# Batch 0's k load moved to the SyncE queue, v and q moved up on the GpSimd queue, in a fused attention and MLP kernel

## The chip, the cores and the metric

One core of one Trainium2 chip. The time is device microseconds of one execution; profiles and stretches are in microseconds from the start of the span. "Granted clock" is the share of TensorE's full clock that the throttle granted. In the profiles PE is TensorE, PEld its weight loads, DVE VectorE, ACT ScalarE, POOL GpSimd and SP SyncE. A "packet" is what one DMA record of the trace moves.

## The reference, cut to what matters

```python
# q, k, v: (8 batches, 8 heads, 576 positions, 64), float32
q_p, k_p = phi(q), phi(k)            # relu, times cos and sin of the position: 128 features
kv  = einsum('bhsf,bhsd->bhfd', k_p, v);  z = sum(k_p, axis=2)
num = einsum('bhsf,bhfd->bhsd', q_p, kv)
den = einsum('bhsf,bhf->bhs', q_p, z)[..., None] + 1e-06
x   = (num / den).transpose(0, 2, 1, 3).reshape(4608, 512)
out = relu(x @ w_in) ** 2 @ w_out    # w_in 512 x 2048, w_out 2048 x 512
```

Nothing of the MLP can start before batch 0's k, v and q have come in and gone through attention.

## The kernel before

576 positions are 4 x 128 and 64 more. Each of k, v and q of a batch is loaded as a main part (1 MB, 4 positions side by side per partition, runs of 1024 bytes in memory) and a "tail" for the last 64 positions (two pieces of 64 KB, runs of 256 bytes).

```python
def load(src, nm, b, eng, parts=1, tail_eng=None):
    main = inp.tile([P, H, J, D], F32, name=nm, tag=nm, bufs=2)
    tail = inp.tile([P, HH, D], F32, name=nm + "t", tag=nm + "t", bufs=2)
    for i in range(parts):
        js = slice(i * J // parts, (i + 1) * J // parts)
        eng.dma_start(out=main[:, :, js, :],
            in_=src[b, :, 0:MAIN, :].rearrange("h (p j) d -> p h j d", j=J)[:, :, js, :])
    for g in range(2):
        (tail_eng or eng).dma_start(out=tail[g * TAIL : (g + 1) * TAIL, :, :],
            in_=src[b, g * HH : (g + 1) * HH, MAIN:S, :].rearrange("h p d -> p h d"))
# ... cut ...
with tc.manual_schedule():
    load(k, "k", 0, nc.gpsimd, 1, nc.sync)
    constants()                               # on GpSimd: iota, identity
    load(v, "v", 0, nc.gpsimd, 1, nc.sync)
    load(q, "q", 0, nc.gpsimd, 2, nc.sync)
    warm(34)                                  # dummy matmuls of 128 x 512, for TensorE's clock
    for j in range(NS):
        att_k(0, j)                           # kp: VectorE (cos) and ScalarE (sin); j = 4 is the tail
    att_v(0, 0, nc.vector)                    # vext: cast of v to bf16
    att_v(0, 1, nc.scalar)
    att_v(0, 2, nc.vector); att_v(0, 3, nc.vector)
    att_v(0, J, nc.vector)                    # vextt, the tail
    for i in range(4):
        load_w1(i, 4)                         # w_in, on GpSimd, cast to bf16 under way
    # ... loads of batch 1, w_out, batch 2, on GpSimd ...
    att_kv(0, 0); att_kv(0, 1)                # kz: 32 matmuls, then 8 that need both tails
    att_feat(0, 0); att_feat(0, 1)            # qp
    att_kvz(0, nc.vector.tensor_copy)         # kvz: kz out of PSUM, needs all 40
    # ... q transposed, num, division, x transposed: xT ...
    for s in range(len(slots)):
        run(s)                                # slots 0 to 3: hps = xT with a quarter of w_in each
```

Each engine keeps this order.

## Time and profile before

| | before |
|---|---|
| time, median (range) of 4 runs | 289.06 us (288.83 to 289.29) |
| span of the profiled run, granted clock | 288.1 us, 0.999 |
| k, v landed (as the casts that wait for them start) | 8.5, 12.07 |
| vextt, kvz start | 13.13, 14.34 |
| first matmul with w_in (slot 0) | 18.51 |
| slot 3, which needs the last quarter of w_in | 25.87 |

How to read it: the page gives busy shares; the chain of waits, followed back from the end, says what the time consists of; the timeline gives start, length, engine, line, operation and, in brackets, the idle time before it and what ended that. "SPq" and "POOLq" are the queues' issues. The lines themselves stand in the prediction below. The profiled execution of this kernel (289.87 us) was slower than the four timed ones. Two paths meet at slot 3: w_in's last quarter, and batch 0's k, v, q through attention into slot 0.

### The profile page before, as it was taken

What the parts mean: (1) busy time and instruction counts of PE and PEld (TensorE: products, weight loads), DVE (VectorE), ACT (ScalarE), POOL (GpSimd) and SP (SyncE); (2) the same over time, 40 slices, a digit from 0 to 9 for tenths busy, and PEclk for the clock granted to TensorE, in tenths of its full rate; (3) what the DMA queues carried; (4) which work ended last, traced back from release to release, by engine and by line L of the source; (5) the groups of instructions that cost most, each with busy time, mean ns of one, the idle gap of its engine ahead of it and who ended that gap; (6) DMA issues with size and microseconds to landing.
All of it is one profiled execution on the core that took longest, in us unless ns stands there. A gap on an engine that the chain in (4) does not pass through costs nothing.

```text
span 288.1 us, 7331 instructions
## 1 busy us (share of the span) xinstructions
PE 278.9 (97%) x3064; PEld 235.9 (82%) x3070; DVE 204.0 (71%) x457; ACT 161.7 (56%) x245; POOL 42.5 (15%) x70
## 2 busy tenths in 40 slices
PE   8699999999999999999999999999999999999995
PEld 3378845888678888898998888888998888889884
DVE  0676774588698399787598776977677877547585
ACT  2675653479759759455882348834695461155210
POOL 8632605750000000000002000000000000000002
PEclk9999999999999999999999999999999999999999
DMA  5999995999658799899529985399809720300015
GB/s 170 343 207 288 322 266 170 369 371 277 91 96 208 142 300 228 219 260 245 167 80 207 333 181 164 94 264 293 231 7 233 118 46 3 136 12 2 0 75 146
DMA packets 74497, 53.04 MB, mean 184 GB/s; under 512 B 52032, under 2 KB 68928, under 8 KB 74464
## 3 DMA queue, kind: packets, MB, share of 16 engines
q1 hardware_dynamic: 63840, 26.09, 40.4%
q0 software_dynamic: 10480, 26.35, 30.0%
q8 instruction: 24, 0.39, 0.5%
q10 hardware_dynamic: 144, 0.13, 0.1%
q14 instruction: 9, 0.07, 0.1%
HBM read 36.70 MB, written 9.44 MB: 160 GB/s over the span
## 4 chain that ended last, share of the span: by engine, by line
PE 85%; DMA 6%; POOL 2%; DVE 2%; ACT 2%; issue 1%; POOLq 0%; ACTq 0%
PE hps L388 40%; PE ya L530 9%; PE yc L530 9%; PE yu L530 7%; DMA w1sb<-in_moe_w_in_dram 6%; PE yv L530 5%; PE num L315 3%; PE kz L243 3%; PE yps L461 2%; PE yps L437 2%; PE yh L437 2%; DVE ysb L542 1%; PE tq L289 1%; POOL w1sb L119 1%; DVE u L542 1%
## 5 line engine op out<-in xcount | busy, mean ns | idle before, releaser
L388 PEld LDWEIGHTS <-w1sb 128*128 128x128 bf16 x1344 | 113.4, 98 | 12.8 <-issue 2.0
L388 PE MATMUL hps<-xT,w1sb 128*128 128x256 bf16 (+1 forms) x1088 | 119.3, 266 | 0.8 <-ACT rt L396 0.2
L396 ACT ACTIVATE rt<-hps 128x1024 bf16<-128x1024 f32 x72 | 73.6, 1023 | 67.6 <-PE hps L388 46.3
L403 DVE TENSOR_TENSOR gT<-rt 128x1024 bf16<-128x1024 bf16 x64 | 44.0, 687 | 19.9 <-ACT rt L396 19.9
L530 PEld LDWEIGHTS <-gs 128*128 128x128 bf16 x480 | 46.8, 98 | 5.4
L415 POOL DMA_DIRECT2D out_dram<-ysb x14 | 7.6, 546 | 171.4 <-DVE ysb L542 144.9
L530 PEld LDWEIGHTS <-gT 128*128 128x128 bf16 x312 | 29.8, 98 | 3.4
L183 ACT ACTIVATE kp<-k,sin_col 128x512 bf16<-128x512 f32 x32 | 22.4, 717 | 5.2 <-DMA k<-in_k_dram 5.2
L329 DVE TENSOR_TENSOR x<-num,rden 128x512 bf16<-128x512 f32 x32 | 22.1, 691 | 1.1
L183 ACT ACTIVATE qp<-q,sin_col 128x512 bf16<-128x512 f32 x32 | 22.0, 719 | 0.8 <-DMA q<-in_q_dram 0.8
L325 DVE TENSOR_SCALAR den<-num 128x8 f32<-128x8 f32 (+1 forms) x40 | 6.5, 164 | 21.5 <-PE num L315 21.4
L526 DVE TENSOR_TENSOR gs<-gT 128x1024 bf16<-128x1024 bf16 x26 | 17.8, 684 | 0.0
L530 PE MATMUL ya<-w2t,gs 128*128 128x256 bf16 x120 | 15.6, 273 | 0.0
L530 PE MATMUL yu<-w2t,gs 128*128 128x256 bf16 x120 | 15.6, 273 | 0.0
L530 PE MATMUL yc<-w2sb,gs 128*128 128x256 bf16 x120 | 15.5, 273 | 0.0
L388 PE MATMUL hps<-xTt,w1sb 128*128 128x128 bf16 x256 | 15.1, 219 | 0.2 <-ACT rt L396 0.2
L173 DVE TENSOR_SCALAR qp<-q,cos_col 128x512 bf16<-128x512 f32 x32 | 15.0, 496 | 0.1
L173 DVE TENSOR_SCALAR kp<-k,cos_col 128x512 bf16<-128x512 f32 x21 | 10.0, 501 | 7.1 <-DMA k<-in_k_dram 7.1
L530 PE MATMUL yu<-w2sb,gs 128*128 128x256 bf16 x112 | 14.5, 273 | 0.0
L202 ACT CAST vext<-v 128x512 bf16<-128x512 f32 x23 | 14.1, 614 | 0.6 <-DMA v<-in_v_dram 0.6
L581 ACT COPY s<-yu 128x256 f32<-128x256 f32 x14 | 5.2, 372 | 15.3 <-PE yu L530 15.3
L530 PE MATMUL yc<-w2sb,gT 128*128 128x256 bf16 x104 | 13.5, 273 | 0.0
(98 smaller groups left out, 336.6 us busy)
## 6 DMA issues: line engine op xcount, KB each, us to landing
out_dram<-ysb POOLq DMA_DIRECT2D x14, 512.0 KB, 4.4
k<-in_k_dram POOLq DMA_DIRECT2D x4, 1024.0 KB, 8.6
v<-in_v_dram POOLq DMA_DIRECT2D x4, 1024.0 KB, 8.6
k<-in_k_dram SPq DMA_DIRECT2D x4, 1024.0 KB, 8.6
v<-in_v_dram SPq DMA_DIRECT2D x4, 1024.0 KB, 8.7
q<-in_q_dram SPq DMA_DIRECT2D x4, 1024.0 KB, 6.6
q<-in_q_dram POOLq DMA_DIRECT2D x3, 1024.0 KB, 12.2
w1sb<-in_moe_w_in_dram POOLq DMA_DIRECT2D x4, 512.0 KB, 14.7
```

What stands on the lines that cost most here:

```text
L173: nc.vector.tensor_scalar(out=dst[:, :, 0:D], in0=src, scalar1=0.0, scalar2=cos_col[:, j : j + 1], op0=ALU.max, op1=ALU.mult,)
L183: nc.scalar.activation(out=dst[:, :, D:F], in_=src, func=ACTF.Relu, scale=sin_col[:, j : j + 1])
L202: copy(out=vx[:, j, h0:h1, 0:D], in_=piece("v", b, j)[:, h0:h1, :])
L243: nc.tensor.matmul(out=kz[:, half, hh * E1 : (hh + 1) * E1], lhsT=lhsT, rhs=rhs, start=(j == 0 and hh == 0), stop=(j == J and hh == HH - 1),)
L315: nc.tensor.matmul(out=out, lhsT=lhsT, rhs=kvz[:, half * HH + hh, :], start=True, stop=True)
L329: nc.vector.tensor_tensor(out=x_of(b, j).rearrange("p (b k) (l d) -> p b k l d", b=n, l=2), in0=n4[:, :, :, 0:D].rearrange("p b (k l) d -> ...
L388: nc.tensor.matmul(out=out, lhsT=w1sb[:, kb, hb * P : (hb + 1) * P], rhs=rhs, start=(kb == 0), stop=(kb == KB - 1),)
L396: nc.scalar.activation(out=rt[:, :, :], in_=hps[:, :, :], func=ACTF.Relu)
L403: nc.vector.tensor_tensor(out=dst, in0=rt[:, :, :], in1=rt[:, :, :], op=ALU.mult)
L437: nc.tensor.matmul(out=ypss[b][tt], lhsT=gTs[b][:, hb, tt * P : (tt + 1) * P], rhs=w2sb[:, hb, :], start=(hb == 0), stop=(hb == HB - 1),)
L526: nc.vector.tensor_tensor(out=t[:, :, :], in0=in0, in1=in1, op=op)
L530: nc.tensor.matmul(out=acc, lhsT=lhs[:, hb, :], rhs=rhs[:, hb, :], start=(hb == 0), stop=(hb == HB2 - 1),)
```

## The change

Its intent: GpSimd needs about 1 us to issue a load, so k is issued by the idle SyncE instead, and v, q and w_in move up. All should land sooner, hence three fewer dummy matmuls.

```diff
     with tc.manual_schedule():
-        load(k, "k", 0, nc.gpsimd, 1, nc.sync)
+        load(k, "k", 0, nc.sync)
+        load(v, "v", 0, nc.gpsimd, 1, nc.sync)
         constants()
-        load(v, "v", 0, nc.gpsimd, 1, nc.sync)
         load(q, "q", 0, nc.gpsimd, 2, nc.sync)
-        warm(34)
+        warm(31)
```

The tails stay on the SyncE queue, but now they stand behind k's 1 MB.

## The prediction

> **What bounds the kernel now.** I read the page first (share of each engine, then the 40 slices), then the chain of waits, the timeline of the first 26 us, the stretches of the same time, and at last the trace's DMA packet records, counted by queue.
>
> ```profile
> span 288.1 us, 7331 instructions
> PE 278.9 (97%) x3064; PEld 235.9 (82%) x3070; DVE 204.0 (71%) x457; ACT 161.7 (56%) x245; POOL 42.5 (15%) x70
> ...
> PE 85%; DMA 6%; POOL 2%; DVE 2%; ACT 2%; issue 1%; POOLq 0%; ACTq 0%
> ```
>
> TensorE bounds all but the start. DMA and POOL together are 8% of the chain, and the chain's list shows them only in the first 26 us, which is the only part that the change touches:
>
> ```profile
> 1.28 1.05 POOL k L66
> 3.51 0.94 POOL v L66
> 4.45 1.75 POOL q L66 x2
> 6.21 2.20 POOL w1sb L119 x3
> 8.41 17.41 DMA w1sb<-in_moe_w_in_dram
> 25.87 1.92 PE hps L388 x16
> ```
>
> The chain blames the w_in load until 25.82. The timeline shows that a second path ends nearly as late: k, v and q of batch 0 must become the first transposed x before the first matmul with w_in at 18.51 can run, and from there TensorE is busy nearly without a gap up to 25.87 (0.2 us of wait for w_in, in the list of waits).
>
> ```profile
> 0.74 1.41 SPq L71 DMA_DIRECT2D kt<-in_k_dram  x2
> 1.20 9.10 PE L208 MATMUL wm<-zeros 128*128 128x512 bf16 x34 [1.20 <-DVE zeros L88]
> 2.20 1.28 SPq L71 DMA_DIRECT2D vt<-in_v_dram  x2
> 8.50 2.56 ACT L183 ACTIVATE kp<-k,sin_col 128x512 bf16<-128x512 f32 x4 [5.21 <-DMA k<-in_k_dram]
> 12.07 1.14 DVE L202 CAST vext<-v 128x512 bf16<-128x512 f32 x3 [1.19 <-DMA v<-in_v_dram]
> 12.55 1.13 PE L243 MATMUL kz<-vext,kp 128*128 128x65 bf16 x32 [2.26 <-DVE vext L202]
> 13.13 0.28 DVE L200 CAST vextt<-vt 128x256 bf16<-128x256 f32 x1
> 14.34 0.69 DVE L254 CAST kvz<-kz 128x520 bf16<-128x520 f32 x1
> 18.51 1.95 PE L388 MATMUL hps<-xT,w1sb 128*128 128x128 bf16 x32
> ```
>
> The dummy matmuls (wm) end at 10.3; TensorE then stands until v is cast. Both paths are fed by the 16 DMA engines:
>
> ```profile
> 2.00:4.50 2.50, 2.50 (x7) 0.91 (x6) 0.00 (x0) 1.23 (x3) 2.18 (x8) 1.00 0.56 117
> 4.50:7.00 2.50, 2.50 (x13) 1.18 (x12) 0.00 (x0) 0.00 (x0) 2.50 (x4) 1.00 0.99 347
> 7.00:8.50 1.50, 1.50 (x9) 0.68 (x7) 0.00 (x0) 0.00 (x1) 1.50 (x3) 1.00 1.06 278
> 8.50:13.50 5.00, 2.74 (x41) 1.64 (x39) 3.70 (x9) 3.58 (x6) 2.55 (x3) 1.00 1.04 380
> 13.50:23.50 10.00, 9.33 (x135) 7.63 (x133) 6.95 (x17) 7.26 (x12) 3.06 (x4) 1.00 1.24 210
> ```
>
> The last two columns are the DMA share and GB/s: the engines are half idle until 4.5 and full after it. (The 210 of the w_in stretch counts bf16 bytes written; twice that is read.)
>
> **What the Trainium skill says.** "DMA: Bandwidth & Descriptors", section "Queues, rings and completion order": each DMA engine goes round robin between the queues with work, at packet granularity. The trace agrees. By queue and size its records give (GpSimd queue: 4096-byte packets; SyncE queue: 256-byte ones for tails, 1024-byte ones for k, v and q):
>
> ```
> us            GpSimd packets        SyncE packets
> 9.0 to 11.0   182 of 4096 B         187 of 256 B      v and q against q's tail
> 165.2-166.0   60 of 4096 B          63 of 1024 B      an output against v of batch 6
> packet alone: 4096 B 160 ns, 1024 B 46 ns, 256 B 18 ns, w_in (1024 B written) 98 ns
> ```
>
> One for one in number, so the queue with the small packets gets a quarter of the bytes or less. Same page, "Issuing engines are not separate DMA queues": another issuing engine only saves issue time. The trace agrees: an issue costs POOL 0.9 to 1.05 us and the bytes still take 2.5 to 3 us per MB. Same page, "Specifications": the first byte comes after about 1 us from GpSimd and 0.6 us from SyncE. Here it is longer but in the same order: tail issued at 0.74, first packet 2.2; k issued at 1.28, first packet 3.4. "TensorE: Matmul & The Clock Gate", "What's actually happening": an idle window of about 3.4 us drops the clock to half. The trace has a 2.26 us gap and keeps its clock at 1.00; no longer gap is there to test it.
>
> **The change, part by part.**
> Removed: k's issue on POOL (1.05 us; k is replaced by v at the same 1.28), and 3 of the 34 dummy matmuls (0.21 us each at the end, 0.65 us; they end at 9.65). Off the path in itself: they ended 2.25 us before they were needed.
> Moved up: v's issue from 3.51 to 1.28, q's and w_in's by 0.94 us. The order of instructions confirms that nothing else moves on POOL, and that TensorE only loses the three.
> Moved over: k's 1 MB to the SyncE queue, in front of all six tail pieces, as 1024 packets of 1024 bytes (64 per engine) instead of 256 of 4096 (16 per engine).
>
> Gain if nothing interferes: k's packets start at about 2.2 instead of 3.4. The engine time until q is done is tails 1536 x 18 ns / 16 = 1.7, k 64 x 0.046 = 2.9, v and q 2 x 16 x 0.16 = 5.1; it was 9.4 with k in large packets, so k costs 0.4 more. Idle share won back in 2.0 to 4.5: 0.44 x 2.5 = 1.1. Net 0.7 to 0.8 us on both paths, and so on the whole.
>
> Loss by round robin. A SyncE load of k in batch 4, issued at 97.66 with no rival, ran at 126 GB/s for its first 2 us (98.5 to 100.5) and 357 after. So by 4.5, when v's packets run at full rate, I take 0.35 MB of k as done: 43 of 64 packets per engine are left. Then:
> v, 16 rounds of 0.16 + 0.046 = 0.205: 3.3 us, to 7.8 (v lands near 9, before 12.04). q the same: to 11.1. k has 11 left, against w_in: 11 x (0.098 + 0.046) = 1.6, to 12.7; with about 1 us to the semaphore, k lands near 13.6, before 8.4.
> The tails stand behind k. Two of k, 32 rounds of 0.098 + 0.018 = 0.116: 3.7 us, to 16.4. Two of v: to 20.1, landing near 20.8, where vextt began at 13.13 before.
> Then vextt 0.28, two casts of q 0.88, so kvz starts near 22.0 instead of 14.34: +7.6. The first w_in matmul would be at 26 instead of 18.5. TensorE would stand from 9.65 to about 17, so its clock may fall: under 1 us more. w_in lands at its old time and takes no part. In the trace before, v's tails slipped through in a dip of the other queue (about 500 packets in 7.0 to 8.0); if they do so again, some 1 to 4 us come back. Estimate of this case: +6.5, range +3 to +9.
>
> **The rivals.**
> (A) k gets through before v is up, the tails slip through the dip between two loads. For: v's first packets were slow (3.4 to 4.5 in the case of k); the lowered count of dummy matmuls says that the author expects an earlier start. Against: the counts above. Result 289.2 - 0.8 = 288.4.
> (B) full round robin as worked out: 289.2 + 6.5 = 295.7. For: two places in the trace with one for one. Against: between 4.8 and 6.6 v's tails stood still beside k at all, so the rule isn't all that is at work.
> (C) k is late by 2 to 4 us only, or k is in time and the tails alone are late: kz waits for its last 8 matmuls. About +3, 292.
> (D) an issue on SyncE delays later work there: its queue has nothing else until 34 us. Nothing.
>
> **Range and chances.** A 0.35, B 0.40, C 0.25: mean 0.35 x 288.4 + 0.40 x 295.7 + 0.25 x 292 = 292.2; I say 292.5 as B can go higher. Range 288.0 to 297.0. 2% slower is 295.0: three quarters of B and a little of C, 0.36. 2% faster is 283.4: there are not 5.8 us to be won in this stretch, 0.02. The rest, 0.62, is within 2%.
>
> **What would show it.** In the timeline: the start of kp (8.50 now; near 13.6 in B, under 8 in A), of the first vext, of vextt (13.13; near 20 in B), of kvz, and of the first w_in matmul (18.51; 26 in B, 17.7 in A). In the packet counts: k's and v's packets one for one between 4.5 and 11. In the waits: in B, ACT and DVE wait for k for 10 us and for the tails after it; in A, the wait for w_in before 25.87 stays. The rest of the trace must be the same, shifted. I am wrong if the shift arises after 30 us, or if k lands late and the span doesn't move.

## The result, and the profile after

The changed kernel: 292.37 us, median of 4 (291.52 to 293.0), against 289.06. The ratio is 1.0113 (95% interval 1.0082 to 1.0143). A ratio is the mean time of one kernel's fast runs over that of the other's in the same rounds, so not quite the ratio of the medians quoted. That is 3.3 us slower, within the 2%. The profiled run (291.97 us, a span of 290.2) was one of its faster ones, and the profiled run of the kernel before one of its slower ones, so the two profiles lie only 2.1 us apart.

The chain of waits of the changed kernel, in order of time (start, length, what):

```profile
3.35 11.68 DMA vt<-in_v_dram
...
15.13 0.31 DVE vextt L200
...
15.48 0.40 PE kz L243 x8
...
21.23 1.79 PE hps L388 x32
...
28.11 1.75 PE hps L388 x16
```

Where the w_in load stood, there is now the load of v's tail: 64 KB that land 11.7 us after their issue. Most of that is waiting in the queue, behind k until 5.7 and then behind three other tail pieces; the four landed at 6.5, 11.1, 13.2 and 15.0. The timeline of the changed kernel:

```profile
0.74 0.45 SPq L66 DMA_DIRECT2D k<-in_k_dram  x1
1.25 1.38 SPq L71 DMA_DIRECT2D kt<-in_k_dram  x2
2.67 1.32 SPq L71 DMA_DIRECT2D vt<-in_v_dram  x2
6.36 2.56 ACT L183 ACTIVATE kp<-k,sin_col 128x512 bf16<-128x512 f32 x4 [3.08 <-DMA k<-in_k_dram]
11.17 0.35 DVE L173 TENSOR_SCALAR kpt<-kt,cos_col 128x256 bf16<-128x256 f32 x1 [1.69 <-DMA kt<-in_k_dram]
11.44 1.13 DVE L202 CAST vext<-v 128x512 bf16<-128x512 f32 x3
15.13 0.30 DVE L200 CAST vextt<-vt 128x256 bf16<-128x256 f32 x1 [2.56 <-DMA vt<-in_v_dram]
16.13 0.69 DVE L254 CAST kvz<-kz 128x520 bf16<-128x520 f32 x1
21.07 1.95 PE L388 MATMUL hps<-xT,w1sb 128*128 128x128 bf16 x32
24.90 0.76 POOL L126 DMA_DIRECT2D w2sb<-in_moe_w_out_dram  x1 [1.78 <-DMA w1sb<-in_moe_w_in_dram]
```

k came in at 6.3 instead of 8.4. The issue of w_out waits for the last quarter of w_in and so shows its landing: it started at 26.10 before and at 24.90 now. (The trace's semaphore events say 25.82 and 24.61.) So for k and v the intent worked: they landed 2.1 and 2.4 us sooner than in this profile of the kernel before, 1.6 us sooner each than in that of run 1. For w_in it isn't shown: in run 1, with the loads as before, the issue of w_out started at 24.91 too. And little of v's gain came through: vext stands behind kpt on VectorE, which waited for k's tail, so it began at 11.44 (before: 12.07, run 1: 11.26). Above all, vextt starts at 15.13 instead of 13.13, TensorE waits 2.4 us for it between the 32nd and the 33rd matmul of kz, and slot 0 starts 2.56 us later. Slot 3 starts at 27.95 instead of 25.87, 2.1 later; it no longer waits for w_in.

The stretches (columns: length, then busy time and count of PE, PEld, DVE, ACT, POOL, then granted clock, DMA share, GB/s). First the kernel before from 27.9 to its end:

```profile
27.90:288.10 260.20, 255.27 (x2825) 219.79 (x2827) 189.34 (x417) 147.46 (x223) 28.42 (x45) 1.00 0.68 177
```

Then the changed one, from 2.1 us later to its end, and two stretches of its start:

```profile
29.98:290.20 260.22, 255.53 (x2830) 219.76 (x2827) 189.27 (x417) 147.46 (x223) 26.38 (x42) 1.00 0.66 173
...
13.00:16.00 3.00, 0.63 (x13) 0.50 (x10) 0.87 (x3) 0.41 (x1) 0.61 (x1) 0.90 1.23 196
16.00:20.00 4.00, 3.77 (x39) 2.99 (x39) 2.96 (x9) 2.40 (x4) 1.54 (x2) 0.65 1.24 203
...
15.38:18.79 3.41, 3.09 (x33) 2.69 (x33) 2.46 (x7) 1.21 (x3) 0.90 (x1) 0.50 1.23 200
```

After slot 3 the two executions last equally long: the whole difference arises before. And TensorE's clock falls there, just where its work is on the path. The 0.65 is a mean over 4 us: the trace's clock record has 0.50 from 15.38 to 18.79 and 1.00 on either side.

The trace's packet records, counted by queue, show why the tail was late:

```
changed kernel, us         GpSimd packets           SyncE packets
before v's first packet    none (v's first: 5.35)   971 of k's 1024, 42 of k's tail
9.0 to 11.0                178 of 4096 B (v, q)     184 of 256 B (tails)
12.5 to 16.5               620 of 1024 B (w_in)     598 of 256 B (tails)
```

(The counts hold to within two packets.) Until k was nearly through, nothing of v moved, although v had been issued at 1.28. After that the tails got one packet of 256 bytes for each of 4096 (later 1024) bytes.

### The profile page after: what moved, and what is told of

The parts are those of the page before. It is cut to its first block, busy times and chain, and to the rows that moved or that the text cites. A ratio compares the mean times of both kernels' runs of the same rounds, so it can differ in the third digit from the quotient of the medians.

```text
span 290.2 us, 7332 instructions
## 1 busy us (share of the span) xinstructions
PE 279.8 (96%) x3067; PEld 236.8 (82%) x3067; DVE 204.7 (71%) x457; ACT 161.6 (56%) x245; POOL 41.5 (14%) x69
## 4 chain that ended last, share of the span: by engine, by line
PE 89%; DMA 4%; DVE 2%; ACT 2%; issue 1%; SPq 1%; ACTq 0%; DVEq 0%
PE hps L388 42%; PE ya L530 9%; PE yc L530 9%; PE yu L530 7%; PE yv L530 5%; DMA vt<-in_v_dram 4%; PE num L315 4%; PE kz L243 3%; PE yps L461 2%; PE yps L437 2%; PE yh L437 2%; PE tq L289 1%; DVE ysb L542 1%; DVE u L542 1%; PE tx L356 1%
## 5 line engine op out<-in xcount | busy, mean ns | idle before, releaser
L173 DVE TENSOR_SCALAR kp<-k,cos_col 128x512 bf16<-128x512 f32 x21 | 11.0, 547 | 4.9 <-DMA k<-in_k_dram 4.9
```

What stands on the lines that cost most here:

```text
L173: nc.vector.tensor_scalar(out=dst[:, :, 0:D], in0=src, scalar1=0.0, scalar2=cos_col[:, j : j + 1], op0=ALU.max, op1=ALU.mult,)
```

## The experiments

All ran on one core and gave right results; they ran in three jobs on three chips, each with the kernel before beside it, and a ratio is to that. Each kernel has one profile. Theory T: the tails of k and v, behind k on the SyncE queue and taking turns one for one, are the loss. Rival C: it is the clock. Rival K: it is k itself on the SyncE queue, through its small packets. The lines of code in these kernels are numbered a few higher.

### 1. The dummy matmuls alone (before_31)

```diff
 # the kernel before
-        warm(34)
+        warm(31)
```

> The kernel before with 31 dummy matmuls instead of 34, the third part of the change alone. TensorE then stands from 9.65 to 12.55, 2.9 us instead of 2.26. Theory: no effect, 289.1 within 0.3 us, clock at 1.00. Rival C: the longer gap lets the clock fall in some runs, 289.5 to 291 with more spread.

289.06 us, ratio 0.9989 (0.9971 to 1.0007), clocks 0.998 and 0.999. No effect. In the profiled run v landed early and the gap ahead of kz was 1.5 us, so the longer gap that was to be tried isn't in that trace. The four times show that three dummy matmuls fewer cost nothing here; what a gap of 2.9 us does to the clock stays untested.

### 2. The tails of k and v behind v on the GpSimd queue (tails_pool)

```diff
 # the changed kernel; the tail loop of load is made a function
-        load(k, "k", 0, nc.sync)
-        load(v, "v", 0, nc.gpsimd, 1, nc.sync)
+        load(k, "k", 0, nc.sync, tails=False)
+        load(v, "v", 0, nc.gpsimd, tails=False)
         constants()
+        load_tail(k, "k", 0, nc.gpsimd)
+        load_tail(v, "v", 0, nc.gpsimd)
         load(q, "q", 0, nc.gpsimd, 2, nc.sync)
```

> The change, but the four tail pieces of k and v of batch 0 are issued on the GpSimd queue behind v's main part instead of on the SyncE queue behind k. Theory T (the tails of v, starved one packet for one behind k on the SyncE queue, are the whole loss): v's tail lands near 10.5 us instead of 15.0, the first w_in matmul starts near 17.1 us instead of 21.1 (18.5 before), the wait for the last part of w_in near 24.7 us sets the rest, no clock drop, and the kernel takes 288.0 us, 1 us under the kernel before. Rival C (the loss is the clock, which falls because TensorE stands in that stretch whatever the tails do): kz ends earlier but the granted clock still falls, 289.5 to 291. Rival K (1024-byte packets of k cost the DMA engines so much that w_in is late): no gain over the changed kernel, 292.

288.58 us, ratio 0.9976 (0.9961 to 0.9992), clocks 0.998 to 1.000. Its timeline:

```profile
11.12 0.35 DVE L178 TENSOR_SCALAR kpt<-kt,cos_col 128x256 bf16<-128x256 f32 x1 [2.70 <-DMA kt<-in_k_dram]
12.59 0.48 DVE L205 CAST vextt<-vt 128x256 bf16<-128x256 f32 x1
18.06 1.95 PE L393 MATMUL hps<-xT,w1sb 128*128 128x128 bf16 x32
```

The tails alone turn a loss of 1.1% into a gain of 0.2%, the clock holds, and K falls: k is on the SyncE queue as in the change. But two things changed at once: on the GpSimd queue the tails also went in larger packets. By 13.1 us its records have 576 packets of 4096 bytes there, 512 for v and q and 64 for the four tail pieces, which on the SyncE queue take 1024 of 256. Place and packet size aren't told apart here. The size of the gain was missed: 17.1 expected for slot 0, 18.06 measured. v landed at 10.31, not 9.64; q's tail, still on the SyncE queue, may have delayed it (in run 9, without it, v landed at 9.80), but k's tail took turns with v in the change too, so this isn't shown. And kpt stands ahead of vext on VectorE, so v waited for k's tail, which was queued behind it.

### 3. Dummy matmuls in the gap (fill_gap)

```diff
 # the changed kernel, in att_kv
         for j in (0, 1) if part == 0 else range(2, NS):
+            if b == 0 and j == J:
+                warm(10)
```

> The changed kernel with ten dummy matmuls put between the second last and the last part of kz, into the 2.4 us in which TensorE waits for v's tail. Theory T with the clock as a second, smaller part: v's tail still lands at 15.0, the granted clock stays at 1.00, the transposes of q after it take 0.2 us less per group of four, the first w_in matmul starts near 20.3 instead of 21.1, and the kernel takes 291.4 us, about 1 us less, with less spread between runs. Rival C (clock is most of it): near 289.5. If the clock plays no part: 292.4.

291.17 us, ratio 1.0072 (1.0049 to 1.0094). Five of six runs held a clock of 1.000 and took 290.89 to 291.25; the sixth, at 0.992, took 292.97. The stretches of the profiled run:

```profile
13.00:16.00 3.00, 2.77 (x22) 1.36 (x22) 1.02 (x4) 0.29 (x1) 0.49 (x2) 1.00 1.23 196
16.00:20.00 4.00, 3.64 (x47) 2.32 (x46) 3.66 (x11) 2.89 (x5) 1.53 (x2) 1.00 1.25 206
```

v's tail came as late as in the change (vextt at 14.98), slot 0 at 20.00. So the clock is 1.0116 - 1.0072 (with run 5 as the change's ratio, from another job), 0.44% or 1.3 us; what is left is 0.72%, 2.1 us, the late tail itself. By an estimate from the intervals of the two ratios the clock is 0.4 to 2.1 us, and without the sixth run, in which it fell all the same, it would be about 1.6; so which part is larger isn't settled. Both T and C are true, with T as the cause of C: in run 2, with the tails in time, the clock held.

### 4. k's load cut into four (k_split)

```diff
 # the changed kernel, in load, for k of batch 0 only
+            for h0 in range(0, H, 2):
+                eng.dma_start(out=main[:, h0 : h0 + 2],
+                    in_=src[b, h0 : h0 + 2, 0:MAIN, :].rearrange("h (p j) d -> p h j d", j=J))
```

> The changed kernel with k's load on the SyncE queue cut into four loads of two heads each, 16 packets per DMA engine instead of 64; all else the same. In the changed kernel v (issued at 1.28) moved nothing until 5.5, when k was done. Theory B (the engine doesn't leave one load's run of up to 64 packets): v's packets start between the pieces, near 3.5, and k lands later, 8 us or more, v near 9.0. Rival R (v's late start comes from the beginning of the GpSimd queue or of v's memory, not from k's run): k lands at 6.3 and v at 9.6 as before. The time changes little in either, 291 to 293, as the tails still come last.

296.07 us, ratio 1.0242 (1.0216 to 1.0267), clocks 0.982 to 0.988. v's first packet came at 3.87, after 549 of k's 1024 (5.35 and 971 in the change); from 5.0 to 7.5 the queues moved 187 packets of v and 142 of k, and k's last came at 10.38 instead of 5.70. The timeline:

```profile
11.06 1.68 DVE L178 TENSOR_SCALAR kp<-k,cos_col 128x512 bf16<-128x512 f32 x4 [9.60 <-DMA k<-in_k_dram]
18.13 0.30 DVE L205 CAST vextt<-vt 128x256 bf16<-128x256 f32 x1 [2.06 <-DMA vt<-in_v_dram]
24.07 1.95 PE L393 MATMUL hps<-xT,w1sb 128*128 128x128 bf16 x32
```

Theory B was right on the mechanism and R falls: cutting k's one long run, 64 packets on each DMA engine, let v in 1.5 us sooner, so it was this run that kept v out. The expectation of the time was wrong by 4 us: k, then its tails, then v's each came later, and both paths wait for the last.

### 5. The changed kernel again (change_again)

> The changed kernel, unaltered, once more on this chip, as the measure for the other three. Every theory: 292.0 to 292.6, granted clock below 1 in its first 25 us.

292.6 us, ratio 1.0116 (1.0095 to 1.0136). Its six runs sort by clock: 291.45 and 291.71 at 0.994, 292.58 at 0.992, 292.62 to 293.63 at 0.988. Kernel and inputs are the same, so the spread goes with how long the clock was down. Its profile, one of the runs at 0.988, has half clock for twice as long as the change's profile (0.994):

```profile
13.92:20.75 6.83, 5.11 (x47) 3.92 (x48) 4.95 (x14) 2.40 (x4) 1.54 (x2) 0.50 1.24 202
```

The kernel before did this rarely: two of its 33 runs beside the experiments had a clock of 0.992, at 290.43 and 290.19 us.

### 6. The tails ahead of k on the SyncE queue (tails_first)

```diff
 # the changed kernel: order on the SyncE queue only
-        load(k, "k", 0, nc.sync)                       # k, kt, then vt, qt
+        load_tail(k, "k", 0, nc.sync)
+        load_tail(v, "v", 0, nc.sync)
+        load_main(k, "k", 0, nc.sync)                  # kt, vt, k, then qt
```

> The changed kernel with only the order on the SyncE queue altered: the tails of k and v are issued before k's main part, not behind it. Theory T (standing behind k on that queue is what makes the tails late): the tails land by 9 us; k is issued some 2.6 us later, near 3.4, so that v's run comes before or amid k's and k lands near 10; kz no longer waits for a tail, the first w_in matmul starts between 17.5 and 19, the clock stays at 1.00, and the kernel takes 288.3 to 289.5, as before the change. Rival K (k on the SyncE queue is itself the loss, through its small packets): 291 or more.

298.27 us, ratio 1.0309 (1.0295 to 1.0322): the slowest of all, where I had expected 289. The tails did land in time (v's by 8.26), but now v was there first (its first packet at 3.54), had the engines nearly to itself (from 4.0 to 6.5 208 of its packets began beside 18 of the tails), and k, behind the tails on its queue, began at 7.03. From 9.0 to 11.5 the records count 180 packets of 4096 bytes on the GpSimd queue against 216 of k's 1024, and k needed until 16.9.

```profile
17.45 2.56 ACT L194 ACTIVATE kp<-k,sin_col 128x512 bf16<-128x512 f32 x4 [14.16 <-DMA k<-in_k_dram]
20.10 0.60 PE L254 MATMUL kz<-vext,kp 128*128 128x65 bf16 x8 [9.42 <-DVE vext L213]
```

So K isn't false everywhere: beside large packets k on the SyncE queue was held up as the tails were. In the change it escaped because its run came first.

### 7. The tails of k and v on ScalarE's queue (tails_act)

```diff
+        load_tail(k, "k", 0, nc.scalar)                # in place of nc.sync, at the start
+        load_tail(v, "v", 0, nc.scalar)
```

> The changed kernel with the tails of k and v issued from ScalarE's own queue at the start, k still first on the SyncE queue. Theory T: the tails land with k or before it, by 7 us, v near 9.7, so that vext no longer waits for kt as it did in the run with the tails on the GpSimd queue; the first w_in matmul starts near 16.8 (18.1 in that run), and the last part of w_in, landing near 24.1, becomes the bound again: 287.7, about 0.9 us under that run's 288.6. Rival: a third queue takes turns with k's run, k lands after 9 us, and nothing is won against the kernel before.

292.08 us, ratio 1.0097 (1.0082 to 1.0111), clocks 0.993 and 0.994. Issued at 0.74, the tails moved nothing until 4.0, while k ran; then three queues took turns (8.5 to 11.0: 209 packets of v and q, 147 of q's tail, 227 of the others), and v's tail landed at 15.2, as in the change:

```profile
15.31 0.29 DVE L205 CAST vextt<-vt 128x256 bf16<-128x256 f32 x1 [2.53 <-DMA vt<-in_v_dram]
```

The expectation (tails by 7) fell. Taking the tails from behind k into a queue of their own wasn't enough, as they still went one for one with large packets. And k's run didn't keep this queue out to its end: from 4.34 to 5.30, before anything of the load behind k began, 187 packets of the tails started beside 282 of k.

### 8. As 7, with q's tail behind w_in on the GpSimd queue (tails_act_qt_late)

> The run before with q's tail moved from the SyncE queue, where it takes turns with v and q, to the GpSimd queue behind w_in. It isn't needed before slot 10. Expected: v and q land 0.3 to 0.5 us earlier and w_in too, 287.4; if two more loads in the GpSimd queue's eight in flight delay w_out or batch 1, it is no faster.

290.32 us, ratio 1.0033 (1.0016 to 1.005). Better than 7 by 1.8 us: with q's tail out of the way v's tail landed at 12.95. But it is short of the expected 287.4 and of the kernel before: in four of its six runs the clock was at 0.993 or 0.994; the two at 0.998 and 1.000 took 289.38 and 289.26.

### 9 to 11. All tails on the GpSimd queue

k's main part stays on the SyncE queue, alone; q's tail goes behind w_in on the GpSimd queue. On that queue, ahead of q and w_in, stand:

```diff
 # tails_pool_qt_late:  v, constants, kt, vt
 # pool_kt_first:       kt, v, constants, vt
 # pool_tails_first:    vt, kt, v, constants
```

> The run with the tails of k and v on the GpSimd queue behind v (288.6), with q's tail too taken off the SyncE queue and put behind w_in on the GpSimd queue, so that k stands alone on the SyncE queue. Theory T2 (any small-packet load that is left on another queue takes one turn for each large packet and delays v): v lands near 9.7 instead of 10.3 and the tails right behind it, the first w_in matmul starts near 17.3 instead of 18.06, the last part of w_in lands near 23.7: 287.9. If it stays at 288.6, the tail of q did no harm, or two more loads among the eight in flight took the gain back.

Run 9, tails_pool_qt_late: 288.99 us, ratio 0.9999 (0.9974 to 1.0025); inconclusive as to time. Its profiled run (287.95) had v at 9.80 and slot 0 at 17.26, as expected, but two of its six runs had clocks of 0.992 and 0.994 and took 290.2; what happened in those two no profile shows.

> As the run above, with k's tail issued on the GpSimd queue ahead of v instead of behind it. k's run on the SyncE queue holds the engines until 5.5 anyway, so v should lose at most 0.3 us; kpt is then done before v lands, and vext starts with v's landing near 9.9 instead of waiting for the tail of k behind it (11.1 in the run of 288.6). First w_in matmul near 17.0; 287.6. Rival: v is issued 1.3 us later and starts later by as much; 288.5.

Run 10, pool_kt_first: 288.09 us, ratio 0.9966 (0.9944 to 0.9989), the fastest: 1 us under the kernel before, 4.3 under the change. The timeline:

```profile
9.75 0.62 ACT L207 CAST vext<-v 128x512 bf16<-128x512 f32 x1 [0.62 <-DMA v<-in_v_dram]
16.33 1.95 PE L393 MATMUL hps<-xT,w1sb 128*128 128x128 bf16 x32
23.89 1.92 PE L393 MATMUL hps<-xT,w1sb 128*128 128x256 bf16 x16 [0.21 <-DMA w1sb<-in_moe_w_in_dram]
```

kz no longer waits for a tail, slot 0 starts 2.2 us sooner than before the change (1.3 sooner than in run 1's profile), and slot 3 waits for w_in again. By this trace attention's path has become the shorter one, so little more should be won by moving attention's loads alone; no run tried it.

> As the run above, with the tails of both v and k ahead of v on the GpSimd queue. v is issued 2.5 us later, near 3.8 to 4.8, and the constants end near 5.9, just before k lands. If v's packets still start by 6.0: first w_in matmul near 16.8, the last part of w_in (near 23.7) is the bound, 287.5. If v's start follows its issue by the 2 us seen for k in the kernel before: v lands near 10.8, 288.5.

Run 11, pool_tails_first: 288.68 us, ratio 0.9984 (0.9963 to 1.0005). v was issued 2.6 us later than in the change and landed at 11.2: the second of the two cases that were expected.

## Why the prediction was right or wrong, point by point

**The time** was right: 292.5 against 292.37, in the range, and within 2%. It came out as a mean of three cases, and the case that happened is C, which had the smallest weight (0.25): k in time and the tails alone late, about +3. C had path and size right; that the mean of the three met the time to 0.13 us is luck.

**The gain if nothing interferes** (0.7 to 0.8 us) was of the right kind: run 10, in which the tails were in time, was 1 us faster than the kernel before. For v the landing moved from 12.04 to 9.64 (11.23 in run 1's profile). For w_in a gain isn't shown: 25.82 became 24.61, but run 1 has 24.63 without the moved loads.

**The step that failed** is the second of the round robin: "by 4.5, when v's packets run at full rate, I take 0.35 MB of k as done", and the sharing of v and k from there. By 4.5 k had moved 669 packets, 0.69 MB, and v moved none until 5.35. k landed at 6.3, not 13.6. The runs show in its place: k, first in time, kept v out until 971 of its 1024 packets were through. In run 4, as four loads of 16 packets per engine, it did so for 549 only; in run 6, with v first, the tails and k behind them waited. Why the first load holds the engines stays open, and it didn't hold them against ScalarE's queue (run 7). I had the sign in hand, under "against" for rival B: v's tails had stood still while k ran in the kernel before.

**The round robin of the tails** was right as a rule: one for one in both stretches counted, though not from the first: from 6.0 to 8.0 160 packets of v began beside 76 of the tails. Their landing, 15.0 instead of 20.8, follows from the failed step: they began behind k at 5, not at 12.7.

**The path from the tail on** was right in kind and nearly 6 us too late for the same reason: kvz started at 16.13, not 22.0. From kvz to slot 0 it then took 4.94 us instead of 4.17, which is the clock: with the clock at 1.00, in run 3, it took 4.02. That kpt would wait for k's tail and hold up vext behind it wasn't foreseen.

**The clock** was an aside ("under 1 us more"). It measures 1.3 us (run 3, with 0.4 to 2.1 by the intervals), and the changed kernel's runs sort by it (run 5).

**w_in "lands at its old time and takes no part"**: it landed 1.2 us sooner than in the profile of the kernel before, at the same time as in run 1's, and indeed took no part.

**Readings of the trace that were off**: k's first packet in the kernel before is at 3.20 in the records, not 3.4; of v's tails about 400 packets, not 500, moved in 7.0 to 8.0; the 31 dummy matmuls ended at 9.99, not 9.65. None of them decides the case.

**Rival D**: right, nothing after slot 3 differs.

**Case B**, 295.7 in the prediction, came near in another kernel: in run 4 v and k did go nearly one for one, k landed at 10.9, slot 0 began at 24.07 instead of 26, and the time was 296.07.

## What to carry to other kernels

Count packets, not bytes, when two DMA queues work at once: small ones on one queue went at the pace of large ones on the other here, and a 64 KB load landed 11.7 us after its issue. Before you move a large load to another queue, look at what stands behind it there and which consumer comes last in program order; here it helped to put small urgent loads into the queue of the large ones, at the place where they are needed, where they also went in large packets. Take a second profile of the unchanged kernel before you call a shift of 1 us a gain. And when a wait grows on the path of TensorE, look whether its clock falls there, as that adds to the wait.

## What the Trainium skill lacked or had wrong

- "DMA: Bandwidth & Descriptors", "Queues, rings and completion order", has round robin at packet granularity. It doesn't say that the packets of the trace are then equal in number and not in bytes (178 to 184, 620 to 598), nor what that does to a small load (four pieces of 64 KB landed one after the other at 6.5, 11.1, 13.2 and 15.0 us, the last 11.7 us after its issue).
- Same section: an engine is said to drain about 9 to 17 descriptors, at most 64, before it turns to another queue. At the start of these runs a load of 64 packets per engine went through whole (971 of 1024 before v's first), and of four loads of 16 about two (549). Later in the same runs the same two queues went one for one (178 to 184). When the one holds and when the other the page doesn't say, and these runs don't settle it.
- Same page, "Issuing engines are not separate DMA queues": another issuing engine is said to save issue time only. Here the queue of the tails moved v's tail from 15.0 to 11.4 (run 2), the order in one queue moved k's landing from 6.3 to 17.4 (run 6), and both moved the whole kernel between 288.1 and 298.3 us, with the same bytes.
- "TensorE: Matmul & The Clock Gate", "HAM oscillation — how this bites in real kernels", names gaps of more than 3.4 us. Here the clock fell to 0.50 for 3.41 us after two gaps of 1.9 and 2.4 us with 1.2 us of matmuls between them, in run 5 for 6.83 us that began within a gap of 2.6, in run 8 for 3.41 us after one of 1.9, and in the kernel before not after one of 2.26 us.
